# Pooled attention and a token/channel mixer on one core: seven-product stage in one more unit, column-tiled token tails, and a rewritten plan

## The chip, the cores and the metric

The kernel runs on one core of one Trainium2 chip. The metric is device time in microseconds of one execution, median of the runs. Engines: TensorE (PE, with weight loads shown as PEld), VectorE (DVE), ScalarE (ACT), GpSimd (POOL), and SyncE (SP), which only issues DMAs here.

## The reference

Eight batches, eight heads, 576 tokens, head size 64. Keys and values are averaged over groups of eight tokens, so that each head attends to 72 keys. The result feeds a mixer: a token layer across the 576 tokens (hidden size 256), then a channel layer across the 512 channels (hidden size 1536), each with a residual.

```
k_p = k.reshape(B, H, Sp, 8, D).mean(axis=3);  v_p likewise
attn = softmax(scale * q @ k_p^T);  x = (attn @ v_p) as (B, S, H*D)
h = relu(x^T @ w_tok1) @ w_tok2;    u = x + h^T
h2 = relu(u @ w_ch1) @ w_ch2;       return u + h2
```

## The kernel before

A batch's 576 tokens are taken as four chunks of 128 and a tail of 64. The work of a batch is cut into named steps: `k0`, `k1`, `v0`, `v1` pool half of the heads on VectorE and `K0` to `V1` the same on GpSimd (`pool`, `pool8`); `kq` pools K on PE by multiplying with the identity (`ppool`); `kpT` transposes the pooled K; `Q0`, `Q1` turn q; `s0` to `s2` are scores and exponentials, eight matmuls tiled by 32 rows (`score4`); `av0` to `av4` are attention times V with the division; `at0`, `at1` the first token layer; `u0` to `u3` the second token layer with its residual, and `u4` that of the tails of two batches at once; `t` and `r` transpose u on PE (evicted on VectorE or ScalarE), and batches from `BOUNCED` = 6 on are turned by `M0`, `M2` (spill to HBM), `M` (load in quarters) and `T0` to `T3` (32x32 block transposes on VectorE).

Batch 0 takes other steps in the head, among them `A0` to `A3`, which finish its transposed u with two matmuls of 512 columns each.

The channel layers are done in nine units: unit n is batch n, and unit 8 is all the tails. A unit has two stages. The first (`first_stage` with `l1_tiles`, or `first_fast`) makes the 12 blocks of the hidden layer `GT`, 512 token columns each; in units 3 to 8, for the groups of `GROUPS`, four blocks are made by seven products on half-size operands instead of eight. The second stage is `unit_plain` (48 matmuls of 512 columns) or, from unit `FAST` on, `unit_fast`: seven products of 12 matmuls of 256 columns each, on sums of weights (`T`, made once by `weight_sum`, tokens `W`) and sums of `GT` (`S`, made in each unit by `g_sums`, tokens `=1a` to `=4b`, or `=10` to `=42` by pairs). S[1] is made from S[0], and S[3] from S[1]. S and T lie in two early buffers, `area` and `area2`, that the head uses for other things. The first stage's own sums are of weights (`%`, `in_weight_sum`) and of tokens (`^`, `token_sum`).

K and V of batches 0 to 3 are loaded as bf16 by GpSimd's DMA queue and pooled in three additions. From batch `SUMMED` = 4 on, a first DMA brings two of the eight rows of a group and three more add to it in flight (`add_rows`, tokens `+`), each waiting for the one before; one addition per half is left.

The order is written out by hand: `HEAD` lists the steps up to unit 0, and `PLANS[n]` says after which yield of unit n's stream of matmuls which steps of other batches are put in. A unit of `unit_fast` yields 23 or so times in its first stage and three times for each product after it. Engines run their instructions in that order, and GpSimd's and SP's DMA issues stand in their queues in that order too. A `<` or `>` ahead of a step shifts its batch.

Of the kernel before, what the change touches and what calls it, by code (L numbers as in the profile page):

```python
# [14 lines left out]
SUMMED = 4  # L15
BOUNCED = 6
FAST = 2
# [11 lines left out]
PLANS = {  # L29
# [32 lines left out]
def kernel(  # L62
# [74 lines left out]
    def pair_sums(b, key):  # L137
        return loaded[b, key].rearrange("j h i d -> j (h i d)").bitcast(FP32)[:, 0:H * 2 * D].rearrange(
            "j (h n) -> j h n", h=H)
# [828 lines left out]
```

## Time and profile before

| | |
|---|---|
| Median of 3 runs | 271.58 us (271.04 to 271.66) |
| Profiled execution | span 269.8 us; no other time is given for it |
| PE, DVE, ACT, POOL busy | 259.5, 206.8, 122.7, 113.4 us |
| Granted TensorE clock | 1.000 |
| DMA | 42081 packets, 35.17 MB, mean 130 GB/s |

```profile
PE   8999999999999999999999999999999999999992
...
DVE  4755573751798859996978798899799889997981
...
POOL 5847749999995428636657242420000000000000
```


The columns of the table come from the page's first lines. The two rows above cut the span into 40 equal slices of 6.7 us; a digit is the engine's busy share in tenths. In the page's other parts, a group of instructions has its line, engine, operation, tiles and shapes, then busy us, mean ns, and the idle time ahead of it with what ended it. Start-to-start times of matmuls are read from the chain, since single matmuls overlap.

### The profile page before, as it was taken

The page shows a single profiled execution, that of the slowest core. Times are in us where ns is not written, and L with a number is a line of the kernel's source. Part 1 is how long each engine was busy: PE and PEld are TensorE (multiplying, and loading weights), DVE is VectorE, ACT ScalarE, POOL GpSimd, SP SyncE. Part 2 cuts the span into 40 slices and gives each one's busy share as a digit, 9 for nine tenths or more (in the row PEclk, how much of TensorE's full clock was granted, in tenths as well). Part 3 has the DMA queues.
Part 4 walks back from the last instruction along what each step waited for, and adds up shares of the span by engine and source line. Part 5 has one row for each costly group of instructions (what it writes and reads, how often), then busy time and mean ns, then how long its engine had stood idle before and what let it go on. Part 6 is the DMA issues. An engine that isn't in the chain of part 4 may idle for free.

```text
span 269.8 us, 5432 instructions
## 1 busy us (share of the span) xinstructions
PE 259.5 (96%) x2173; PEld 171.7 (64%) x2200; DVE 206.8 (77%) x427; ACT 122.7 (45%) x207; POOL 113.4 (42%) x114
## 2 busy tenths in 40 slices
PE   8999999999999999999999999999999999999992
PEld 2776454545544645776587657864785688787781
DVE  4755573751798859996978798899799889997981
ACT  1375773047444353736563637264922632613600
POOL 5847749999995428636657242420000000000000
PEclk9999999999999999999999999999999999999999
DMA  7999999959969898998995997361506510404106
GB/s 184 190 194 205 204 212 204 180 126 190 153 132 140 154 159 118 146 169 168 155 141 83 156 213 87 39 164 40 119 0 147 149 18 21 137 2 116 41 2 157
DMA packets 42081, 35.17 MB, mean 130 GB/s; under 512 B 12040, under 2 KB 34408, under 8 KB 42056
## 3 DMA queue, kind: packets, MB, share of 16 engines
q0 software_dynamic: 30672, 22.11, 55.3%
q1 hardware_dynamic: 11056, 12.39, 17.2%
q10 hardware_dynamic: 328, 0.33, 0.5%
q8 instruction: 17, 0.28, 0.4%
q14 instruction: 8, 0.07, 0.1%
HBM read 36.90 MB, written 10.49 MB: 176 GB/s over the span
## 4 chain that ended last, share of the span: by engine, by line
PE 90%; DVE 5%; ACT 2%; issue 1%; DVEq 0%
PE p L777 24%; PE p L561 22%; PE p L695 9%; PE p L592 8%; PE p L453 6%; PE p L468 5%; PE p L357 4%; PE p L391 3%; PE p L862 3%; PE p L480 2%; PE p L323 1%; DVE area L614 1%; DVE u L470 1%; ACT ex L379 1%; ACT x L426 1%
## 5 line engine op out<-in xcount | busy, mean ns | idle before, releaser
L564 ACT ACTIVATE GT<-p 128x512 bf16<-128x512 f32 x76 | 44.5, 596 | 57.6 <-PE p L561 43.7
L561 PE MATMUL p<-uT,w_ch 128*128 128x512 bf16 x274 | 69.3, 380 | 0.9 <-issue 0.4
L561 PEld LDWEIGHTS <-w_ch 128*128 128x128 bf16 x304 | 32.4, 114 | 24.1 <-issue 1.7
L362 ACT ACTIVATE ex<-p 72x1024 bf16<-72x1024 f32 (+1 forms) x42 | 31.6, 804 | 27.5 <-PE p L357 27.3
L777 PEld LDWEIGHTS <-area 128*128 128x128 bf16 x336 | 31.9, 98 | 5.3 <-issue 1.3
L777 PE MATMUL p<-area,area 128*128 128x256 bf16 x252 | 30.8, 273 | 0.0
L145 POOL DMA_DIRECT2D kr<-in_k_dram x16 | 23.4, 1495 | 15.6 <-DMA kr<-in_k_dram 15.6
L145 POOL DMA_DIRECT2D vr<-in_v_dram x16 | 23.1, 1478 | 14.2 <-DMA vr<-in_v_dram 14.2
L470 DVE TENSOR_TENSOR u<-p,x 128x512 bf16<-128x512 f32 x32 | 21.1, 680 | 8.2 <-PE p L468 8.2
L777 PEld LDWEIGHTS <-GT 128*128 128x128 bf16 x252 | 24.2, 98 | 4.9 <-issue 0.6
L592 PE MATMUL p<-w_ch,GT 128*128 128x512 bf16 x92 | 23.6, 379 | 0.2
L777 PE MATMUL p<-w_ch,GT 128*128 128x256 bf16 x168 | 20.6, 273 | 0.1
L799 DVE TENSOR_TENSOR o<-p,s 128x512 f32<-128x512 f32 (+1 forms) x28 | 17.9, 662 | 3.2 <-PE p L777 3.1
L396 DVE TENSOR_TENSOR x<-p,den 128x512 bf16<-128x512 f32 x28 | 19.4, 691 | 1.0
L468 PE MATMUL p<-AT,w_tok 128*128 128x512 bf16 x62 | 17.3, 379 | 0.5 <-DVE u L470 0.5
L799 DVE TENSOR_TENSOR s<-p,u 128x512 f32<-128x512 f32 x24 | 16.2, 680 | 2.0 <-PE p L777 2.0
L395 DVE RECIPROCAL den<-p 128x8 f32<-128x8 f32 (+1 forms) x35 | 7.0, 201 | 11.3 <-PE p L391 10.9
L391 PEld LDWEIGHTS <-ex 72*128 72x128 bf16 x280 | 12.6, 98 | 3.9 <-DVE x L396 0.2
L592 PEld LDWEIGHTS <-GT 128*128 128x128 bf16 x96 | 8.8, 98 | 9.4 <-issue 0.4
L453 PE MATMUL p<-x,w_tok 128*128 128x512 bf16 x53 | 13.7, 379 | 0.2
L446 ACT ACTIVATE AT<-p 128x512 bf16<-128x512 f32 x14 | 8.4, 597 | 12.1 <-PE p L453 11.7
L391 PE MATMUL p<-vp,ex 72*128 72x65 bf16 x280 | 13.7, 194 | 0.0
(151 smaller groups left out, 448.8 us busy)
## 6 DMA issues: line engine op xcount, KB each, us to landing
out_dram<-o SPq DMA_DIRECT2D x34, 256.0 KB, 3.8
kr<-in_k_dram POOLq DMA_DIRECT2D x16, 288.0 KB, 7.4
vr<-in_v_dram POOLq DMA_DIRECT2D x16, 288.0 KB, 7.0
qb<-in_q_dram POOLq DMA_DIRECT2D x7, 576.0 KB, 10.1
kr<-in_k_dram POOLq DMA_DIRECT2D x3, 576.0 KB, 10.9
vr<-in_v_dram POOLq DMA_DIRECT2D x3, 576.0 KB, 12.4
w_ch<-in_moe_w_ch_dram POOLq DMA_DIRECT2D x6, 256.0 KB, 10.6
w_ch<-in_moe_w_ch_dram POOLq DMA_DIRECT2D x3, 512.0 KB, 13.1
```

Of the source, the lines that this page charges most:

```text
L145: nc.gpsimd.dma_start(out=pair_sums(b, key), in_=src[:, :, 2 * i * D:2 * (i + 1) * D], accum_op=ALU.add if i else ALU.bypass)
L362: nc.scalar.activation(out=exv[:, a, :, gs[0]:gs[-1] + 1, n0:n0 + n], func=AF.Exp, scale=scale, in_=pss[a][0:SP, :, 0:len(gs) * n].rearran ...
L391: nc.tensor.matmul(out=ps[:, h // 4, (h % 4) * (D + 1):(h % 4 + 1) * (D + 1)], lhsT=st["ex"][:, h * S + n0:h * S + n0 + P], rhs=st["vp"][: ...
L453: nc.tensor.matmul(out=ps, lhsT=w_tok1[:, c if c < 4 else 4 + par, m * P:(m + 1) * P], rhs=st["x"][:, c, :] if c < 4 else st["xt"], start= ...
L468: nc.tensor.matmul(out=ps, lhsT=w, rhs=a, start=(i == 0), stop=(i == len(mms) - 1))
L470: nc.vector.tensor_tensor(out=quads_of(dst, on), in0=plain_of(ps, on), in1=plain_of(x, on), op=ALU.add)
L561: nc.tensor.matmul(out=ps[m], lhsT=w_ch1[m // 4][:, kk, m % 4:512:4], rhs=moving(u)[kk], start=(kk == 0), stop=(kk == 3))
L564: nc.scalar.activation(out=GT[:, m, :], in_=ps[m], func=AF.Relu)
L592: nc.tensor.matmul(out=ps, lhsT=GT[:, m, c * P:(c + 1) * P], rhs=w_ch2[:, m, :], start=(m == 0), stop=(m == NM - 1))
L695: nc.tensor.matmul(out=ps[:, i], lhsT=w(i, k), rhs=mv(k), start=start and (i, k) == (0, 0), stop=stop and k == 1, skip_group_check=True)
L777: nc.tensor.matmul(out=ps[i] if split else ps[:, i], lhsT=a(m)[:, i * P:(i + 1) * P], rhs=w(m), start=start and m == 0 and (i == 0 or spli ...
L799: nc.vector.tensor_tensor(out=dst, in0=src, in1=other[:, i], op=ALU.add)
```

## The change

- `FAST` = 1: unit 1's second stage is `unit_fast`, so the sums of `w_ch2` are made in unit 1.
- In `unit_fast` the products come in the order GT lo, GT second half, S[1], S[0], S[2], S[3], GT hi; the buffer `s4` and its addition are gone, and the last product adds u directly.
- `u4` uses 64-column tiles of the second token layer's weights at two column positions instead of the zero-padded `w_tok2t`, which is gone.
- `BOUNCED` = 5: batch 5 is turned through HBM too.
- `ROWS`: K and V of batches 4 to 7 come in two DMAs of four rows, the second adding to the first; two additions per half are left.
- K of batch 1 is pooled on VectorE (`k0:1`, `k1:1`), not by `kq0`, `kq1` on PE; the K halves of batches 2 and 3 go from GpSimd to VectorE. `kpA` evicts the transposed keys on ScalarE.
- `#` and `~` do sums of GT and of tokens on GpSimd; `=` and `^` on VectorE as before.
- `HEAD` has 13 warm-up matmuls for 26, K of batch 0's first heads in two smaller DMAs, and another order.
- `PLANS` is replaced throughout; steps name their batch after a colon, and `do` runs them.
- The last unit stores its parts as they come, its last part in two transfers.

The core of the diff, with the plan of a few units:

```
-SUMMED = 4
-BOUNCED = 6
-FAST = 2
+ROWS = {4: 4, 5: 4, 6: 4, 7: 4}
+BOUNCED = 5
+FAST = 1
...
-HEAD = """z Z d2 Lc d5 d2 Lk8 d2 d2 d1 d2 d2 d1 d1 R0 c1 c0 I Lk1 Lq Lv0 Lv8 Lv1 kf0 Lf Lb La R1 d1 kf1 Bk1 H0 d1
-          d4 q1 kt0 kt1 q0 kp2 kp3 o0 e0 kt2 kt3 q2 q3 o1 e1 P0 vp0 o2 e2 a00 a01 a02 vp1 o3 e3 P1 y00 y01 y02 y03
-          y04 b10 X0 X1 a11 a12 A1 A0 y10 y11 y12 y13 y14 X2 X3 Bq1 Bv1 P2 H1 H2 Bk2 Ld G0"""
+HEAD = """Sk0 S80 z Sq0 Sk1 Sq1 N z0 R0 Z Lc d1 d1 d1 d1 d1 d1 d1 d1 d1 d1 d1 d1 d1 I kf0 c0 Lk1 kT0 p0 Lk8 c1 Lq
+          e0 o0 kf1 kt1 Lv8 Lv0 q1 kp2 kt2 Lv1 p3 La Lf kp3 q2 o1 kt3 e1 vP0 e2 e3 o2 a00 a01 vp1 o3 P1 a02 Lb X1
+          X0 Bk1 H0 P0 b10 y00 y01 a12 Bq1 a11 y02 y10 y03 y04 H1 y11 R1 Bv1 X2 A1 k0:1 y12 y13 A0 y14 H2 Ld X3
+          A3:0"""
...
-    1: {1: "s1", 5: "+k3a", 8: "av1", 10: ">K0", 16: ">K1 av2", 17: "av3", 18: "lk4", 20: ">Q0 s2", 21: ">Q1",
-        22: "av0", 23: "av4", 25: ">kpT", 27: "lq4", 29: "at1 >V1 at0", 30: "W10", 34: ">v0 >s1 u1", 35: "u3",
-        37: "W11 >s0 t3 W02 +v3b u0", 40: "u2", 41: "+k3b t0", 42: "W00 t2 >s2", 45: "t1 lv4 %01", 46: "W01 >av4"},
...
+    1: {
+        0: "W00 lv:3", 1: "W12 W02", 3: "W01", 9: "W10 lq:3", 11: "s1:2", 12: "=3a", 13: "W03", 16: "W11",
+        17: "k0:3 k1:3", 18: "=1a s2:2", 21: "av1:2", 23: "kpA:3 =2a", 24: "=1b av0:2", 25: "+v:4 +k:4",
+        28: "#2b av3:2", 29: "av4:2", 30: "#4a", 31: "av2:2", 32: "=3b Q0:3 Q1:3", 33: "W13 V1:3",
+        35: "at1:2 at0:2 =4b lq:5 s0:3", 36: "u1:2", 37: "u3:2", 38: "s2:3", 39: "u2:2 s1:3 t3:2 V0:3", 40: "u0:2",
+        41: "r2:2", 42: "r0:2 lq:4", 43: "t1:2 av4:3",
+    },
+    2: {
...
+    4: {
+        1: "at0:5 Q0:6 at1:5 Q1:6", 3: "k0:6", 4: "^14 K1:6 u2:5 u0:5 u1:5", 6: "Q0:7", 7: "~24", 10: "t4:1",
+        11: "M0:5 %61", 12: "V0:6 ~34 kpA:6", 15: "u3:5", 19: "=3b V1:6 lv:7 =3a =1a", 20: "s0:6", 21: "#2a",
+        23: "=1b", 25: "s2:6 u4:5", 26: "#2b", 27: "s1:6", 29: "#4b", 32: "av4:6 M2:5", 34: "av0:6", 35: "#4a M:5",
+        37: "T0:5", 38: "r4:3 T2:5 T1:5", 39: "T3:5 %62 av2:6", 43: "+v:7 av3:6",
+    },
+    5: {
...
+    8: {
+        2: "~38", 17: "=11", 18: "=12 =32", 21: "=21 =22", 22: "=10 =20", 26: "#30 =31", 27: "#40", 36: "#41 #42",
+    },
...
-    w_tok2t = singles.tile([P, 2, 2, P], BF16)
...
-        nc.gpsimd.dma_start(out=pair_sums(b, key), in_=src[:, :, 2 * i * D:2 * (i + 1) * D],
+        nc.gpsimd.dma_start(out=pair_sums(b, key), in_=src[:, :, ROWS[b] * i * D:ROWS[b] * (i + 1) * D],
...
-                if b < SUMMED:
+                if b not in ROWS:
                     pool8(eng, loaded[b, t], hs, dst, t == "k")
                     return
-                pair = pair_sums(b, t)[:, hs].rearrange("j l (i n) -> i j l n", i=2)
+                rows = pair_sums(b, t)[:, hs]
+                if ROWS[b] == 4:
+                    eng.tensor_tensor(out=rows[:, :, 0:2 * D], in0=rows[:, :, 0:2 * D], in1=rows[:, :, 2 * D:4 * D], op=ALU.add)
+                pair = rows[:, :, 0:2 * D].rearrange("j l (i n) -> i j l n", i=2)
...
-        def kpT():
+        def kpT(act=False):
...
+            (nc.scalar.copy if act else nc.vector.tensor_copy)(
+                out=st["kD"].rearrange("p g e j -> p (g e j)"), in_=ps.rearrange("p i j -> p (i j)"))
...
-                    mms = [(w_tok2t[:, m, half, :], tails[b // 2, half][:, m, :]) for half in range(2) for m in range(2)]
+                    mms = []
                     dst, x = u_tails[:, b // 2, :], st["xt"]
+                    for m in range(2):
+                        for half in range(2):
+                            rows = slice(half * BP, (half + 1) * BP)
+                            nc.tensor.matmul(out=ps[rows], lhsT=w_tok2[:, m, 8 * BP:S], rhs=tails[b // 2, half][:, m, :],
+                                             start=(m == 0), stop=(m == 1), tile_position=(0, half * BP))
...
+    def sub(out, a, b, eng=nc.vector):
+        eng.tensor_tensor(out=out, in0=a, in1=b, op=ALU.subtract)
...
-    def token_sum(n, u, i):
+    def token_sum(n, u, i, eng):
...
-        def store_part(cols):
-            def go(i):
-                if i == 0:
-                    return
-                for half in range(2):
-                    dst = out.rearrange("(c h) (p r) n -> h p c r n", h=2, r=BR)[half]
-                    (nc.scalar if half else nc.sync).dma_start(out=dst[:, 2:4, 8, cols],
-                                                               in_=ob[half * BP:(half + 1) * BP, :, cols])
-            return go
+        def store_part(g, o, cols, i):
+            for half in range(2):
+                dst = out.rearrange("(c h) (p r) n -> h p c r n", h=2, r=BR)[half]
+                (nc.scalar if half else nc.sync).dma_start(out=dst[:, 2 * g:2 * g + 2, 8, cols][:, i],
+                                                           in_=o[half * BP:(half + 1) * BP, i, cols])
...
-        yield from product(y, lambda m: GT[:, NH + m, lo], lambda m: w_ch2[:, NH + m, lo], True, plus(oa[:, :, lo], y, s1))
+        both = slice(0, 2)
+
+        def stored(g, o, cols):
+            return (lambda i: i == 0 or store_part(g, o, cols, both)) if last else None
+
+        yield from product(y, lambda m: GT[:, NH + m, lo], lambda m: w_ch2[:, NH + m, lo], True,
+                           plus(oa[:, :, lo], y, s1, stored(0, oa, lo)))
+        s2 = keep("s1")
+        yield from product(x, lambda m: SG[:, 1, m], lambda m: TW[:, 1, m], False, plus(s2, x, u1hi), last)
         z = bank()
         s5 = keep("s5")
         yield from product(z, lambda m: SG[:, 0, m], lambda m: TW[:, 0, m], True, plus(s5, z, u2hi))
-        s2 = keep("s1")
-        yield from product(x, lambda m: SG[:, 1, m], lambda m: TW[:, 1, m], False,
-                           plus(s2, x, u1hi), last)
+        yield from product(x, lambda m: SG[:, 2, m], lambda m: TW[:, 2, m], False,
+                           plus(ob[:, :, hi], x, s5, stored(1, ob, hi)), last)
+        yield from product(z, lambda m: SG[:, 3, m], lambda m: w_ch2[:, NH + m, hi], False,
+                           plus(oa[:, :, hi], z, s2, stored(0, oa, hi)))
         if not last:
-            w = bank()
-            s4 = keep("s4")
-            yield from product(w, lambda m: GT[:, NH + m, hi], lambda m: TW[:, 3, m], True, plus(s4, w, u2lo))
-        yield from product(z, lambda m: SG[:, 3, m], lambda m: w_ch2[:, NH + m, hi], False, plus(oa[:, :, hi], z, s2))
-        store(n, 0, oa)
-        if last:
-            yield from product(x, lambda m: SG[:, 2, m], lambda m: TW[:, 2, m], False,
-                               plus(ob[:, :, hi], x, s5, store_part(hi)), True)
-            yield from product(x, lambda m: GT[:, NH + m, hi], lambda m: TW[:, 3, m], False,
-                               plus(ob[:, :, lo], x, u2lo, store_part(lo)), True)
-        else:
-            def finish(i):
-                plus(ob[:, :, hi], x, s5)(i)
-                plus(ob[:, :, lo], x, s4)(i)
-            yield from product(x, lambda m: SG[:, 2, m], lambda m: TW[:, 2, m], False, finish)
+            store(n, 0, oa)
+        yield from product(x, lambda m: GT[:, NH + m, hi], lambda m: TW[:, 3, m], False,
+                           plus(ob[:, :, lo], x, u2lo, (lambda i: store_part(1, ob, lo, i)) if last else None), last)
+        if not last:
             store(n, 1, ob)
...
+        elif s[0] == "S":
+            a = int(s[2])
+            if s[1] == "q":
+                nc.sync.dma_start(out=qf[:, a:a + 1, :], in_=q_pairs(a, a + 1))
+            elif s[1] == "8":
+                kv(kf, k, 0, 0, HP, BP, SP, nc.scalar)
+            else:
...
+    def do(s):
+        if s[0] == "W":
+            weight_sum(int(s[1]), int(s[2]))
+        elif s[0] == "%":
+            in_weight_sum(int(s[1]), int(s[2]))
+        elif s[0] in "^~":
+            b = int(s[2])
+            token_sum(b, batches[b][2] if b < B else dict(uT=uT_tails), int(s[1]), nc.vector if s[0] == "^" else nc.gpsimd)
+        elif s[0] in "=#":
+            g_sums(s[1:], nc.vector if s[0] == "=" else nc.gpsimd)
```

More of the change, by code (lines that the diff above doesn't have):

```diff
@@ L137, in pair_sums @@
     def pair_sums(b, key):
-        return loaded[b, key].rearrange("j h i d -> j (h i d)").bitcast(FP32)[:, 0:H * 2 * D].rearrange(
+        return loaded[b, key].rearrange("j h i d -> j (h i d)").bitcast(FP32)[:, 0:H * ROWS[b] * D].rearrange(
             "j (h n) -> j h n", h=H)
@@ L187, in permute_tok2 @@
             return
-        for half in range(2):
-            nc.gpsimd.tensor_copy(out=w_tok2t[:, :, half, half * BP:(half + 1) * BP], in_=w_tok2[:, :, 8 * BP:S])
     def load_ch1(g):
@@ L338, in go @@
                                         in_=loaded[b, "q"][:, hp, rr * P:(rr + 1) * P], identity=ident)
-                nc.vector.tensor_copy(out=qT0[:, hp].rearrange("m l (r p) -> m r l p", p=BP), in_=ps)
+                (nc.scalar.copy if act else nc.vector.tensor_copy)(
+                    out=qT0[:, hp].rearrange("m l (r p) -> m r l p", p=BP), in_=ps)
             return go
@@ L890, in head @@
             nc.vector.memset(w_tok1[:, 4:6, :], 0.0)
-            nc.vector.memset(w_tok2t, 0.0)
         else:
             batches[0][1][s]()
+    def do(s):
[8 more added lines that the diff above has]
+            g_sums(s[1:], nc.vector if s[0] == "=" else nc.gpsimd)
+        elif ":" in s:
+            s, b = s.split(":")
+            if s[0] == "l":
+                load(s[1], int(b))
+            elif s[0] == "+":
+                add_rows(int(b), s[1])
+            else:
+                batches[int(b)][1][s]()
+        else:
+            head(s)
     def unit(n, at):
@@ L903, in unit @@
             for s in at.get(i, "").split():
-                if s[0] == "W":
-                    weight_sum(int(s[1]), int(s[2]))
-                    continue
-                if s[0] == "%":
-                    in_weight_sum(int(s[1]), int(s[2]))
-                    continue
-                if s[0] == "^":
-                    b = int(s[2])
-                    token_sum(b, batches[b][2] if b < B else dict(uT=uT_tails), int(s[1]))
-                    continue
-                if s[0] == "!":
-                    head(s[1:])
-                    continue
-                if s[0] == "=":
-                    g_sums(s[1:])
-                    continue
-                if s[0] == "l":
-                    load(s[1], n + int(s[2]))
-                    continue
-                if s[0] == "+":
-                    if SUMMED <= n + int(s[2]) < B:
-                        add_rows(n + int(s[2]), s[1])
-                    continue
-                ahead = {"<": 0, ">": 2}.get(s[0], 1)
-                s = s.lstrip("<>")
-                if n + ahead < B and ((n + ahead) % 2 or s not in ("u4", "t4", "r4")):
-                    batches[n + ahead][1][s]()
+                do(s)
     with tc.manual_schedule(engines={PE, POOLE, DVE, ACT, SYNC}):
@@ L934 @@
         for s in HEAD.split():
-            head(s)
+            do(s)
         for n in range(B + 1):
```

44 lines of the change are left out of this document (26 added, 18 removed), and 45 rows, old and new, of the table PLANS.

## The prediction

> **What bounds the kernel now.** I read the page first, then the stages, the waits of TensorE, the chain of waits, the groups by shape and the timeline at a few places.
>
> ```profile
> PE 259.5 (96%) x2173; PEld 171.7 (64%) x2200; DVE 206.8 (77%) x427; ACT 122.7 (45%) x207; POOL 113.4 (42%) x114
> ...
> PE 90%; DVE 5%; ACT 2%; issue 1%; DVEq 0%
> ```
>
> TensorE (PE) is busy for 259.5 of 269.8 us and carries 90% of the chain that ended last. A busy share can hide waits inside pipelined matmuls, so I look at stages (start:end, share of PE, weight loads, VectorE, ScalarE, GpSimd in us) and at the waits of PE.
>
> ```profile
> 0.00:23.45 23.45, 20.95 (x189) 13.89 (x191) 14.15 (x43) 11.26 (x23) 15.62 (x29) 1.00 1.07 192
> 23.45:58.85 35.40, 34.79 (x253) 18.40 (x256) 20.79 (x39) 15.03 (x24) 27.44 (x25) 1.00 1.08 196
> 58.85:89.14 30.29, 29.92 (x236) 15.01 (x238) 19.76 (x36) 14.99 (x24) 25.02 (x20) 1.00 0.92 149
> 89.14:119.10 29.96, 29.25 (x253) 19.09 (x256) 25.77 (x51) 14.68 (x24) 17.21 (x15) 1.00 1.00 137
> ...
> 175.27:205.31 30.04, 29.93 (x273) 19.86 (x275) 28.01 (x57) 16.33 (x28) 1.60 (x2) 1.00 0.34 86
> ```
>
> ```profile
> PE p L862 <- DVE area L881: 1.2, 1, 1.2
> PE p L413 <- ACT ex L379: 0.6, 2, 0.4
> PE p L468 <- DVE u L470: 0.5, 1, 0.5
> ```
>
> The stretches are head, units 0, 1, 2 and 5. From unit 0 on PE misses at most 0.7 us in a unit, and its longest wait for another engine after the head is 0.5 us. In unit 5 VectorE is busy for 28.01 of 30.04 us and PE still does not wait. So what a removed matmul is worth is its place in the stream, start to start, and what other engines gain or lose is worth nothing until one falls behind PE. The chain gives those places:
>
> ```profile
> 24.91 0.88 PE p L323 x8
> ...
> 54.70 0.58 PE p L357 x8
> ...
> 57.54 0.45 PE p L480 x8
> ...
> 98.82 0.88 PE p L468 x4
> ...
> 131.01 2.16 PE p L561 x10
> ...
> 217.43 9.17 PE p L777 x84
> ```
>
> A 512-column matmul takes 2.16/10 = 0.216 us, a 256-column one 0.109 to 0.110, a 128-column transpose 0.056.
>
> **The change part by part.** The plan is rewritten as a whole, so I take PE's removed work term by term and then ask of each other engine whether it keeps up. The counts come from comparing the two instruction streams.
>
> *Seven products in unit 1.* 48 matmuls of 512 columns (L592) become 84 of 256: 48 x 0.216 = 10.37 against 9.17 from the row of 84. Gain 1.2 us. VectorE pays three more output adds (7 for 4) and eight sums of GT halves, of which six stay on it; the eight sums of w_ch2 were made before too, only later. Unit 1 has the room: 19.76 busy of 30.29.
>
> *K of batch 1 off TensorE.* 16 matmuls of 256 columns with the identity (L323, kr) go: 2 x 0.88 = 1.76 us. VectorE gets two half pools of three operations instead of two copies.
>
> *Batch 5 turned via HBM.* 16 transposes go: 2 x 0.45 = 0.9 us. The turn adds two spills, four loads on SP's queue and four 32x32 block transposes on VectorE. Batches 6 and 7 do the same now and their units start without a wait, so I cost it at nothing else. SP's queue holds only stores beside it.
>
> *Token tails.* Four times, four matmuls with a zero-padded weight (0.88 us on the chain) become two pairs of 64-column tiles. Nothing in this trace is tiled by columns; the nearest row is the scores', tiled by rows: eight 512-column matmuls in 0.58 us, where two rounds of four would be 0.43 and one after another 1.73. So tiles overlap and a change of tiling costs about 0.15. For a pair-wise tail that is 0.43 + 0.15 = 0.58, a gain of 0.30 each and 1.2 in all. The ends are 4 x 0.43 = 1.7 gained if the change of tiling is free, and 4 x 0.15 = 0.6 lost if the pairs do not overlap. I take 1.1, since the two halves feed different moving data through the same rows, which the scores do not do. The Trainium skill, TensorE: Matmul & The Clock Gate, Part 3, gives 2.38 times the speed for three column tiles; two at that efficiency (an estimate) would be 1.6 times, 0.55 us a tail, 1.3 gained. The Trainium skill, TensorEngine Tiling (Array Packing), Restrictions, speaks against: column tiling switches the fast weight load off. No row here shows that; weight loads overlap other matmuls, so the sum does not use it.
>
> *The head.*
>
> ```profile
> 5.75 1.14 DVE L302 TENSOR_TENSOR GT<-GT 72x512 f32<-72x512 f32 x2 [2.53 <-DMA GT<-in_k_dram]
> ...
> 9.58 0.44 PE L337 MATMUL p<-ident,qb 128*128 128x128 bf16 x5
> ...
> 12.64 0.71 POOL L194 DMA_DIRECT2D w_ch<-in_moe_w_ch_dram  x1 [1.00 <-DMA vr<-in_v_dram]
> ...
> 23.45 0.59 PE L561 MATMUL p<-uT,w_ch 128*128 128x512 bf16 x2
> ```
>
> ```profile
> w_ch<-in_moe_w_ch_dram POOLq DMA_DIRECT2D x6, 256.0 KB, 10.6
> ```
>
> The K of the first heads comes in two smaller loads and PE's first useful work needs only the first, with 13 warm-up matmuls for 26: perhaps 3 us sooner than 9.58. But the DMA engines are full in this stage (share 1.07), and unit 0 needs w_ch1, whose second load was issued at 12.64 and takes a median of 10.6: about 23.2. Unit 0 began at 23.45, and some steps of batch 0 stood after that (two of the A steps, 0.86 us), which can now be done before. The gain lies between nothing and some 2.5 us; I take 0.7, nearest to the row of w_ch1.
>
> *K and V from two halves.* 32 accumulating loads of two rows become 16 of four.
>
> ```profile
> L145 POOL DMA_DIRECT2D kr<-in_k_dram x16 | 23.4, 1495 | 15.6 <-DMA kr<-in_k_dram 15.6
> ...
> L218 POOL TENSOR_TENSOR t<-t 72x512 f32<-72x512 f32 x8 | 10.3, 1288 | 0.7
> ...
> L217 POOL TENSOR_TENSOR t<-vr 72x1024 f32<-72x1024 bf16 x4 | 8.5, 2133 | 1.8 <-DMA vr<-in_v_dram 1.7
> L277 POOL TENSOR_TENSOR vp<-vr 72x256 bf16<-72x256 f32 x8 | 8.5, 1067 | 6.1 <-DMA vr<-in_v_dram 6.1
> ...
> L614 DVE TENSOR_TENSOR area<-GT 128x768 bf16<-128x768 bf16 x10 | 6.1, 611 | 0.0
> ...
> L217 DVE TENSOR_TENSOR t<-vr 72x1024 f32<-72x1024 bf16 x2 | 3.5, 1745 | 0.0
> ...
> L221 POOL TENSOR_TENSOR kp<-t 72x256 bf16<-72x256 f32 x4 | 3.3, 836 | 0.3
> ...
> L614 DVE TENSOR_TENSOR area<-GT 128x512 bf16<-128x512 bf16 x6 | 2.5, 416 | 0.7 <-ACT GT L564 0.7
> ...
> L218 DVE TENSOR_TENSOR t<-t 72x512 f32<-72x512 f32 x2 | 1.8, 896 | 0.1
> ...
> L223 DVE TENSOR_TENSOR vp<-t 72x256 bf16<-72x256 f32 x2 | 0.8, 424 | 0.1
> ```
>
> GpSimd saves 16 issues x 1.495 = 24 us, and its waits for landings get fewer. It pays ten more adds of 512 elements, 13 us.
>
> *Replaced work.* GpSimd loses the K pools of batches 2 and 3 (four halves, 2.13 + 1.29 + 0.84 = 4.3 us each) and gets 24 sums of GT and 14 token sums: 19 of 768 elements at about 1.7 (between 1.288 and 2.133), 19 of 512 at 1.29, 57 us. Its total comes to about 113 - 24 + 13 - 17 - 6 (six pair adds of 1.07 that go to VectorE) + 57 = 136 of some 265 us, now spread over all units. VectorE gives those 38 sums (19 x 0.61 + 19 x 0.42 = 20 us), six score-key copies and six output adds, and takes the six K half pools of batches 1 to 3 (1.745 + 0.896 + 0.42 = 3.1 each, 18 us), six adds of later halves and four block transposes. Its sum changes by about 2 us. Unit by unit, with these prices, I get VectorE at 31 against PE 32 in unit 0, 28 against 29 in unit 1, 24 to 26 against 27 to 29 in units 2 to 5, 16 against 21 in unit 6: tightest early, looser than before from unit 4 on (unit 5 was 28.01).
>
> *The new order in the second layer.* The product on S[1] moves one product (1.31 us) forward, while its second half needs a chain: last relu on ScalarE, a sum on VectorE (0.61), and in units 1 and 4 a sum on GpSimd (1.7). In unit 1 that is
>
> ```profile
> L564 ACT ACTIVATE GT<-p 128x512 bf16<-128x512 f32 x76 | 44.5, 596 | 57.6 <-PE p L561 43.7 <-DVE o L799 8.9 <-issue 4.4
> ```
>
> the last matmul 0.2, the relu 0.6, the sums 0.6 and 1.7, plus hand-overs, 3.5 to 4, against two products and three attention steps on PE, 2.6 + 0.8 = 3.4, so a wait of 0 to 0.5 there; behind it stand all later matmuls of the unit. In unit 4 two more score steps lie before it. In unit 8 the last sums of S[3] run on GpSimd, three of 1.29 in a row against 6.5 us of PE work. I charge 0.6 for such waits in all.
>
> *The end.*
>
> ```profile
> 264.62 0.42 DVE L799 TENSOR_TENSOR o<-p,u_tails 128x256 f32<-128x256 f32 x1 [0.23 <-PE p L777]
> ```
>
> ```profile
> out_dram<-o SPq DMA_DIRECT2D x2, 128.0 KB, 3.8
> ```
>
> The last product stays, and its last store of 128 KB is halved; from that add to the end 269.8 are 5.2 us, of which a smaller transfer may save 0.1.
>
> **Sum.** 1.2 + 1.76 + 0.9 + 1.1 + 0.7 + 0.1 - 0.6 = 5.2 us off the span: 269.8 - 5.2 = 264.6. The page gives the profiled execution by its span alone; the median of the timed runs, 271.58, is 1.8 over it. With the same 1.8 the forecast is 266.4.
>
> **The rivals.**
>
> *VectorE falls behind PE because GpSimd holds it up (slower).* This is the strongest objection:
>
> ```profile
> 100.29 2.09 POOL L277 TENSOR_TENSOR kp<-kr 72x256 bf16<-72x256 f32 x2 [4.63 <-DMA kr<-in_k_dram]
> ...
> 101.60 1.19 DVE L614 TENSOR_TENSOR area<-GT 128x768 bf16<-128x768 bf16 x1
> ...
> 105.09 0.55 DVE L614 TENSOR_TENSOR area<-GT 128x768 bf16<-128x768 bf16 x1
> ```
>
> The same sum takes 0.55 alone and 1.19 beside a GpSimd sum: both read SBUF twice, and each waits for the other. After the change GpSimd computes for roughly a third of the time (136 us less some 50 of DMA issues, of 265), and VectorE has some 60 us of such SBUF operations (40 sums of GT and 10 of tokens, 26 us; eight half pools alone at about 2.3, 19; six later halves, 7; weight sums, 10): a third of 60, about 20 us of lengthening. Spread out, VectorE still stays under PE. It decides from the point at which it comes together in unit 1 (28 us of VectorE against 29 of PE, with w_ch2 sums, K pools and two V pools of GpSimd side by side): 6 us more there is 34 against 29, 5 us of waiting, and 1 us in each of units 3 to 5: 8 us, so 266.4 + 8 = 274.4. The Trainium skill, GPSIMD Engine Reference, Engine selection and Key points, advises the same way: two-input elementwise work belongs on VectorE, GpSimd is about twice as slow and shares SBUF interfaces with it. By that rule, the trace agrees (1.7 to 0.55, and the 1.19). Against it: unit 5 ran at 28.01 of 30.04 with no wait of PE.
>
> *The small gains fail (still faster).* Column tiles do not overlap, the head keeps w_ch1's date, and PE waits 1.5 us for sums: 1.2 + 1.76 + 0.9 - 0.6 + 0.1 - 1.5 = 1.9 off, 269.7.
>
> *The head gives all it could (faster).* If the earlier first work and the freed queue bring unit 0 forward by 2.5 us: 266.4 - 1.8 = 264.6; with free tiling changes and no waits for sums 263.4.
>
> *Unit 1's seven products wait for their weights' sums.* If the third load of w_ch2, which now is queued behind K of batch 2, delays unit 0's second layer, or the sums in `area2` are late by about 5 us, nothing is left: 271.6. The bytes ahead of that load are the same as before, which speaks against it.
>
> **How the numbers follow.** Forecast 0.57, around 265 to 268; small gains fail 0.14; head gives all 0.10; unit 1's weights 0.05; VectorE behind 0.14. A measurement of this kernel tells a change from none at about 0.3%, 0.8 us. Faster by more than that: 0.57 + 0.14 + 0.10 = 0.81, of which I move 0.02 to slower for waits that no row shows; so 0.79 faster, 0.05 same, 0.16 slower. The range runs from 263.0, a little under the head's best case, to 271.0, just short of no change, and leaves out about 0.2.
>
> **What would show it.** In the profile after: no L323 on kr for batch 1; 84 more 256-column matmuls in unit 1 and none of 512 at the plain layer beyond unit 0; each tail at about 0.6 us on the chain; PE's waits after the head below 0.5 us each and its busy sum down by 5 or more; unit 0's first matmul of the channel layer between 21 and 23.5. I am wrong if PE waits for VectorE or GpSimd by more than 3 us in units 1 to 5, if L614 and the pools on VectorE lengthen to over 1.0 us on average, or if unit 0 starts later than 23.5.

## The result: 1.0 us gained of the 5.2 forecast

The median over 20 runs each is 270.55 us after (268.19 to 272.95) against 271.58 before (270.51 to 272.64). The ratio is 0.9949, 95% interval 0.9929 to 0.9969: 0.5% faster, far less than forecast. The three longest executions after (272.23 to 272.95) belong to a slower state and are not in the ratio. The profiled execution of the changed kernel is the longest of its 20, 272.95 us with a span of 271.1; why shows below. The page after:

```profile
PE 258.2 (95%) x2191; PEld 173.3 (64%) x2191; DVE 216.6 (80%) x415; ACT 125.2 (46%) x213; POOL 133.7 (49%) x126
...
PEclk9856999999999999999999999999999999999999
```

GpSimd's sum came out as worked out (133.7 for about 136). New is the row of the granted clock, full in every slice of before. The stages after, units 0 to 4 in the same columns as in the prediction, with the granted clock third from the right:

```profile
0.00:30.32 30.32, 24.17 (x179) 16.86 (x180) 15.60 (x42) 14.13 (x27) 17.49 (x30) 0.77 1.08 187
30.32:63.49 33.17, 32.61 (x233) 15.81 (x232) 27.71 (x46) 14.01 (x24) 11.99 (x11) 1.00 1.03 183
63.49:93.30 29.81, 29.19 (x275) 18.27 (x274) 26.81 (x48) 17.75 (x29) 21.44 (x19) 1.00 0.85 138
93.30:121.61 28.31, 28.31 (x257) 18.37 (x255) 22.81 (x46) 14.23 (x23) 16.20 (x15) 1.00 0.88 177
121.61:150.88 29.27, 28.25 (x280) 19.82 (x279) 26.83 (x46) 14.01 (x23) 22.43 (x20) 1.00 0.86 155
```

Unit 0 begins at 30.32 instead of 23.45, and the clock in the head is 0.77. From there to TensorE's last matmul it takes 236.3 us instead of 241.1, and from that to the end 4.4 instead of 5.2: nearly all that was hoped for is there, and the head takes 6.9 back. The timeline of TensorE in the head (start, length, then the idle time before and what ended it):

```profile
4.58 1.30 PE L887 MATMUL p<-area 128*128 128x512 bf16 x5
6.20 0.30 PE L337 MATMUL p<-ident,area 72*128 72x72 bf16 x4 [0.32 <-DVE area L329]
...
7.58 0.65 PE L401 MATMUL p<-area 128*72 128x320 bf16 x4 [0.80 <-ACT area L364]
...
10.43 0.61 PE L317 MATMUL p<-kr,ident 72*72 72x128 bf16 x8 [1.69 <-DMA kr<-in_k_dram]
11.55 0.42 PE L337 MATMUL p<-ident,area 72*128 72x72 bf16 x4 [0.52 <-DVE area L320]
12.26 0.71 PE L362 MATMUL p<-ident,qb 128*128 128x128 bf16 x5 [0.29 <-DMA qb<-in_q_dram]
```

The warm-ups (L887) end before 6 us, and in the next 6.5 us TensorE waits five times, 3.6 us in all, for K, q and their evictions. The clock records of this trace read: 1.0 for 6.83 us from 4.68, then 0.5 for 13.65 us from 11.51, then 1.0 to the end. Before there was one record, 1.0. Executions differ in how much of this they have: mean clocks and times of four runs after are 1.000 and 268.19 us, 0.991 and 268.83, 0.984 and 271.02, 0.975 and 272.95.

### The profile page after: what moved, and what is told of

It reads as the page before. It is cut to its first block, busy times and chain, and to the rows that moved or that the text cites. A ratio compares the mean times of both kernels' runs of the same rounds, so it can differ in the third digit from the quotient of the medians.

```text
span 271.1 us, 5481 instructions
## 1 busy us (share of the span) xinstructions
PE 258.2 (95%) x2191; PEld 173.3 (64%) x2191; DVE 216.6 (80%) x415; ACT 125.2 (46%) x213; POOL 133.7 (49%) x126
## 4 chain that ended last, share of the span: by engine, by line
PE 80%; DVE 13%; DMA 2%; issue 1%; POOL 1%; ACT 0%; DVEq 0%
PE p L808 23%; PE p L592 22%; PE p L726 8%; PE p L499 5%; PE p L479 5%; PE p L623 4%; PE p L383 3%; PE p L417 3%; DMA qb<-in_q_dram 2%; DVE o L830 2%; PE p L511 2%; DVE t L695 1%; DVE x L422 1%; PE p L348 1%; PE p L401 1%
## 5 line engine op out<-in xcount | busy, mean ns | idle before, releaser
L808 PEld LDWEIGHTS <-area 128*128 128x128 bf16 x384 | 35.9, 98 | 6.2 <-issue 0.9
L808 PE MATMUL p<-area,area 128*128 128x256 bf16 x288 | 36.1, 273 | 0.0
L808 PEld LDWEIGHTS <-GT 128*128 128x128 bf16 x288 | 27.1, 98 | 7.6 <-issue 2.5
L645 POOL TENSOR_TENSOR area<-GT,area 128x768 bf16<-128x768 bf16 (+1 forms) x12 | 17.7, 1492 | 26.0 <-DVE area L645 26.0
L808 PE MATMUL p<-w_ch,GT 128*128 128x256 bf16 x192 | 24.0, 273 | 0.0
L830 DVE TENSOR_TENSOR o<-p,s 128x512 f32<-128x512 f32 (+1 forms) x25 | 16.5, 664 | 4.9 <-PE p L808 4.6
L645 POOL TENSOR_TENSOR area<-area,GT 128x768 bf16<-128x768 bf16 x4 | 6.5, 1632 | 25.4 <-DVE area L656 25.4
L645 POOL TENSOR_TENSOR area<-GT 128x768 bf16<-128x768 bf16 (+1 forms) x7 | 11.5, 1649 | 12.2 <-ACT GT L595 6.7
L830 DVE TENSOR_TENSOR s<-p,u 128x512 f32<-128x512 f32 x21 | 14.4, 686 | 3.4 <-PE p L808 3.4
L417 PEld LDWEIGHTS <-ex 72*128 72x128 bf16 x280 | 13.5, 98 | 3.3
L656 DVE TENSOR_TENSOR area<-GT 128x768 bf16<-128x768 bf16 (+1 forms) x17 | 8.5, 507 | 6.8 <-ACT GT L595 6.8
L808 PE MATMUL p<-w_ch,area 128*128 128x256 bf16 x96 | 12.8, 273 | 0.3 <-DVE area L645 0.3
```

What stands on the lines that cost most here:

```text
L417: nc.tensor.matmul(out=ps[:, h // 4, (h % 4) * (D + 1):(h % 4 + 1) * (D + 1)], lhsT=st["ex"][:, h * S + n0:h * S + n0 + P], rhs=st["vp"][: ...
L645: eng.tensor_tensor(out=out, in0=a, in1=b, op=ALU.subtract)
L808: nc.tensor.matmul(out=ps[i] if split else ps[:, i], lhsT=a(m)[:, i * P:(i + 1) * P], rhs=w(m), start=start and m == 0 and (i == 0 or spli ...
L830: nc.vector.tensor_tensor(out=dst, in0=src, in1=other[:, i], op=ALU.add)
```

## The experiments

Four questions, a comparison of three or four kernels for each: what the clock costs; where the gain of the head and of unit 0 went; what each piece of removed matmul work is worth; which version is best. My theory to begin with was the clock; the rivals were the order of the head and VectorE held up by GpSimd. The kernel before, run beside them, took 271.52, 271.58, 271.27 and 271.39 us in the four comparisons.

### The clock

**26 warm-ups again**, in a row, all else as in the change:

```
-... Lc d1 (13 times) I kf0 ...
+... Lc d1 (26 times) I kf0 ...
```

> The changed kernel with 26 warm-up matmuls in a row for 13; they end near 8.3 us instead of 5.5. Clock theory (the shorter warm-up leaves TensorE idle in the head, its clock is halved for one or two periods of 6.8 us and unit 0 starts late): granted clock 1.000 in every run, unit 0's first matmul of the channel layer near 25 us instead of 30.3, time 266.5 to 268. Rival (the new head's order and its loads make it late, the clock follows from that and costs little): clock may rise, but time stays 269.5 to 271.

Measured: 269.08 us, ratio 0.9909 [0.9886, 0.9932]; clocks 0.997 to 1.0. The head and unit 0:

```profile
0.00:25.20 25.20, 20.68 (x192) 13.74 (x194) 15.38 (x42) 13.81 (x27) 16.13 (x28) 1.00 1.07 189
25.20:58.36 33.16, 32.39 (x229) 15.82 (x232) 27.70 (x46) 14.01 (x24) 13.38 (x13) 1.00 1.15 207
```

The rest is as after, to 0.02 us in each unit up to unit 6. Of the 6.9 us that the profiled head lost, 5.1 are the clock; over all executions it is 270.55 - 269.08 = 1.5. But unit 0 still begins at 25.20.

**The gaps filled**: 13 early warm-ups kept, 15 more put where TensorE waited, so that no real work comes later.

```
-Lq e0 o0 kf1 kt1 Lv8 Lv0 q1 kp2 kt2 Lv1 p3
+Lq d4 e0 o0 kf1 kt1 Lv8 Lv0 q1 d7 kp2 d2 kt2 Lv1 d2 p3
```

> The changed kernel with 15 more warm-up matmuls, put where TensorE waits in the head (4 before the first scores, 7 before the first K pool on TensorE, 2 and 2 after it). Clock theory: clock 1.000, and as they fill waits only, 266 to 267.5, as fast as with 26 in a row or a little faster. Rival (order and loads): 269.5 to 271, as the late loads are not touched.

Measured: 268.90, ratio 0.9900 [0.9877, 0.9923]; clocks 0.998 to 1.0. Unit 0 begins at 25.61. Both ways of keeping TensorE busy bring the clock back, so idleness it is. Neither brings unit 0 to 23.5.

**The other way round**: the kernel before with its last 13 warm-ups dropped.

```
-d2 d2 d1 d2 d2 d1 d1 R0 ... R1 d1 kf1 Bk1 H0 d1 d4 q1
+d2 d2 R0 ... R1 kf1 Bk1 H0 q1
```

> The kernel before with 13 of its 26 warm-up matmuls (the later ones left out), nothing else. Clock theory: TensorE idles from about 5.5 to 9.4 us, the clock is halved for some runs, 272.5 to 275.5 and a wide scatter. Rival: no loss, 271 to 272, since its order of the head is untouched.

Measured: 271.86, ratio 1.0012 [0.9993, 1.0032]; clocks 0.982 to 0.996. Its trace has a wait of 2.2 us behind the warm-ups and one half-clock record of 6.83 us (7.88 to 14.7). So the halving is not special to the new plan. In the profile unit 0 begins 1.3 later than in the kernel before; in the medians it costs only 0.3 us, within what can be told from nothing.

**The head of before** on the new kernel, with its warm-ups and its order (one larger K load excepted, which the new steps take in two):

```
-HEAD = """Sk0 S80 z Sq0 Sk1 Sq1 N z0 R0 Z Lc d1 ... X0 Bk1 H0 P0 b10 ... H2 Ld X3 A3:0"""
+HEAD = """z Sk0 Sk1 S80 Sq0 Sq1 N z0 Z d2 Lc d5 d2 Lk8 ... X2 X3 Bq1 Bv1 k0:1 H1 H2 Ld A3:0"""
```

> The changed kernel with the order and warm-ups of the head before (26 warm-ups, both copies of q first), the split loads and the steps that the new plan needs kept. Clock theory: clock 1.000, unit 0 near 23 to 24 us, 266 to 267.5. Rival: the same, and 2 us or more faster than the new head with 26 warm-ups or filled gaps.

Measured: 268.93, ratio 0.9912 [0.9889, 0.9935], the same as with 26 warm-ups alone. Unit 0 begins at 24.71 and ends at 58.73, where it ended at 58.36 with the new order and at 58.69 in the kernel before. In the medians the order of the head decides nothing. The end of unit 0 has hardly moved, though 2.8 us of matmul work and waiting were to go from the head and unit 0; how long the warm-ups themselves took in each profile is in these ends too, and is reckoned with further down.

### Where the gain of unit 0 went

With the gaps filled, the third load of `w_ch2` is late, as one of the rivals had it, but by 0.8 us, not 5 (waits of TensorE: total, count, longest):

```profile
PE p L623 <- DMA w_ch<-in_moe_w_ch_dram: 0.8, 1, 0.8
```

**That load ahead of K of batch 2**, the gaps filled as before (all of this comparison starts from it):

```
-7: "u3:0 G1", ... 20: "av2:1 G2"
+7: "u3:0 G1 G2", ... 20: "av2:1"
```

> The kernel with filled gaps, and the third load of w_ch2 issued ahead of K of batch 2, not behind it. Theory (with a full clock the rest of the missing gain is TensorE waiting 0.8 us or more in unit 0's second stage for that load): the wait in front of L623 goes, 267.5 to 268.3, and no new wait for K of batch 2. Rival (the 1 us of scatter comes from elsewhere): 268.9 as with filled gaps alone.

Measured: 271.76, ratio 1.0011 [0.9987, 1.0036]: 2.9 us lost. The wait for `w_ch` is gone, and this stands in its place, in the timeline of VectorE and in the waits of TensorE:

```profile
49.54 1.22 DVE L238 TENSOR_TENSOR t<-kr 72x1024 f32<-72x1024 bf16 x1 [2.83 <-DMA kr<-in_k_dram]
...
54.40 0.69 DVE L501 TENSOR_TENSOR u_tails<-p,xt 128x512 bf16<-128x512 f32 x1
```

```profile
PE p L499 <- DVE u_tails L501: 2.3, 1, 2.3
```

K of batch 2 lands later, VectorE waits 2.83 us for it with both half pools at the head of its queue, and the eviction that TensorE needs stands behind these until 54.40. In the kernel before, GpSimd pooled this K, and its waiting held up no eviction.

**The tails padded again**, with `w_tok2t` back, on the same kernel:

```
-nc.tensor.matmul(out=ps[rows], lhsT=w_tok2[:, m, 8 * BP:S], rhs=tails[b // 2, half][:, m, :], ...
+mms = [(w_tok2t[:, m, half, :], tails[b // 2, half][:, m, :]) for half in range(2) for m in range(2)]
```

> As with w_ch2 early, but the token tails of two batches again in one zero-padded matmul each. If the column tiles overlap as the trace says (four matmuls in about 0.55 us for 0.86), this is 1.2 us slower than the run with w_ch2 early; if TensorE has slack in those units, less than 0.5.

Measured: 272.32, ratio 1.0038 [1.0011, 1.0066], 0.6 over the kernel it starts from, with overlapping intervals. The profiles are sharper: units 2, 4 and 6 are 0.32, 0.31 and 0.20 us longer, the other units from 1 on the same to 0.01.

**All sums on VectorE**: the 24 sums of GT and 14 of tokens that GpSimd had taken.

```
-28: "#2b av3:2", 29: "av4:2", 30: "#4a", ...   41: "~23",
+28: "=2b av3:2", 29: "av4:2", 30: "=4a", ...   41: "^23",
```

> As with w_ch2 early, but the 24 sums of GT and 14 token sums of GpSimd are back on VectorE, at the same places of the order. Theory A (GpSimd's sums hold VectorE up and cost TensorE 1 to 3 us in units 1 and 3): faster by 0.5 to 2 us. Theory B (VectorE would be the bound without that help): slower by 2 us or more, with waits for VectorE in units 4 to 8.

Measured: 287.36, ratio 1.0575 [1.0528, 1.0621]: 15.6 us more. Its page and the waits of TensorE:

```profile
PE 262.0 (92%) x2206; PEld 171.4 (60%) x2206; DVE 234.0 (82%) x453; ACT 125.0 (44%) x213; POOL 83.0 (29%) x88
```

```profile
PE p L808 <- DVE area L645: 3.8, 4, 1.4
PE p L499 <- DVE u_tails L501: 3.6, 1, 3.6
```

VectorE is busy only 82% of the span, and TensorE waits for it all the same. This trace also has two stretches of 3.41 us at half clock, from 54.9 and from 85.7 us, so at most 3.4 of the 15.6 are the clock. GpSimd's help is what carries the new plan.

**Three steps moved** where VectorE was late in units 0, 1 and 3:

```
-1: "G0 A2:0 kpT:1"                      +1: "G0 A2:0", 3: "kpT:1"
-32: "=3b Q0:3 Q1:3" 35: "... =4b lq:5"  +32: "=3b Q0:3" 34: "=4b" 36: "Q1:3 lq:5 ..."
-8: "%21" (unit 3)                       +27: "%21" (unit 2)
```

> As with w_ch2 early, and three steps moved: the transposes of batch 1's keys two yields later, the last sum of S[3] ahead of the second turn of q in unit 1, one sum of w_ch1 from unit 3 to unit 2. The stalls seen in the trace (0.6 in unit 0, about 1.2 in unit 1, 1.2 in unit 3) should go: 1.5 to 2.5 us faster than with w_ch2 early, 265.5 to 266.5. Rival (they only move on to the next wait): under 0.5 us.

Measured: 269.16, ratio 0.9914 [0.9882, 0.9946], 2.6 us under the kernel it starts from. Unit 1 fell from 29.81 to 28.83 us, unit 3 from 29.26 to 28.09, and unit 2 rose from 28.31 to 29.15, 1.3 in sum; the other 1.3 of the profile lies ahead of unit 1, which begins at 61.14 for 62.46. What VectorE and GpSimd did in units 1 and 3 is in the timeline of the kernel with the gaps filled:

```profile
81.33 2.14 POOL L238 TENSOR_TENSOR t<-vr 72x1024 f32<-72x1024 bf16 x1
...
81.52 2.37 DVE L645 TENSOR_TENSOR area<-GT,area 128x768 bf16<-128x768 bf16 x1
...
83.95 0.28 PE L808 MATMUL p<-w_ch,area 128*128 128x256 bf16 x1 [0.31 <-DVE area L645]
...
84.55 0.38 PE L499 MATMUL p<-AT,w_tok 128*128 128x512 bf16 x1 [0.32 <-DVE u L501]
```

```profile
122.26 2.43 DVE L695 TENSOR_TENSOR t<-w_ch,w_ch 128x512 bf16<-128x512 bf16 x1
...
122.97 1.17 POOL L645 TENSOR_TENSOR t<-uT,t 128x512 bf16<-128x512 bf16 x1
...
125.59 0.38 PE L479 MATMUL p<-x,w_tok 128*128 128x512 bf16 x1 [1.03 <-DVE x L422]
```

A sum of 0.55 us alone takes 2.37 beside GpSimd's V pool, and in the lines behind it TensorE waits. In unit 3 it is `%21`, a sum of weights that could be made at another time, ahead of the eviction of x. This is the slower rival's mechanism, at about 2 us in two units instead of 8 in four.

### What each piece is worth

**More moves**, on the last kernel: K of batch 2 pooled four or five yields later, `A2:0` ahead of `k1:1`, `%21` in the middle of unit 2.

```
-28: "av4:1 k1:2 lv:2", 29: "at1:1 at0:1 k0:2"   +28: "av4:1 lv:2", ... 32: "k1:2", 34: "k0:2 lk:3"
-0: "k1:1", 1: "G0 A2:0"                         +0: "A2:0", 1: "G0 k1:1"
-27: "%21" (unit 2)                              +14: "%21" (unit 2)
```

> Filled gaps, w_ch2 early, the local moves, and two more: VectorE pools K of batch 2 four to five yields later, so that its wait for that load has fewer evictions behind it, and batch 0's last A step goes ahead of the pool of batch 1's K. Theory (a late load costs TensorE only by what stands behind the waiting instruction in VectorE's queue): the waits of 2.3 us in unit 0 and 0.7 in unit 2 go, 265.8 to 267.0, the fastest version. Rival (the loads themselves are late for TensorE): 268 to 269.

Measured: 270.78, ratio 0.9989 [0.9965, 1.0012]. A miss. Unit 2 is at 28.31 with `%21` in it, as expected, but the later pools cost more in unit 0 than they gave:

```profile
PE p L499 <- DVE o L631: 2.2, 1, 2.2
PE p L307 <- DVE kp L242: 1.7, 1, 1.7
```

It is the base of the next three.

**Unit 1's second stage plain**, with the sums of w_ch2 made in it still:

```
-FAST = 1    (unit 1: "=3a", "=1a", "=2a", "=1b", "#2b", "#4a", "=3b", "=4b")
+FAST = 2    (unit 1: none of these)
```

> As all moves, with unit 1's second layer in 48 matmuls of 512 columns and without its eight sums of GT. Predicted term: 1.2 us slower than all moves. If VectorE and GpSimd were what limits unit 1, it is less than 0.5 slower or even faster.

Measured: 272.95, ratio 1.0038 [1.0014, 1.0061], 2.2 over its base. Unit 1 takes 30.02 us for 28.83: 1.19, the predicted 1.2 to a hundredth. The rest of the difference lies in unit 0, in which this edit changes nothing: this trace has half clock for 3.41 us there, from 57.29 to 60.70, just behind TensorE's wait of 2.2 us for VectorE, and the base's trace, with the same wait, has none. Eight of the 12 executions here have a mean clock of 0.994 or less, and four of the base's 12; the medians of the others, 271.3 and 270.4, are 0.9 apart.

**K of batch 1 on TensorE again**:

```
-... A1 k0:1 y12 ...   0: "A2:0", 1: "G0 k1:1"
+... A1 kq0:1 y12 ...  0: "A2:0", 1: "G0 kq1:1"
```

> As all moves, with K of batch 1 pooled by TensorE again (16 matmuls of 256 columns and two copies) and not on VectorE. Predicted term: 1.8 us slower than all moves. If VectorE's pools stand in the way in unit 0, it is less than 0.8 slower.

Measured: 270.88, ratio 0.9993 [0.9970, 1.0016]: 0.1 more than its base. The 1.76 us of removed matmuls bring nothing here.

**Batch 5 turned on TensorE again**:

```
-BOUNCED = 5   11: "M0:5 %61" 32: "av4:6 M2:5" 35: "#4a M:5" 37: "T0:5", 38: "r4:3 T2:5 T1:5", 39: "T3:5 ..."
+BOUNCED = 6   11: "%61"      32: "av4:6"      35: "#4a"     37: "r0:5", 38: "r4:3 r2:5 t1:5", 39: "t3:5 ..."
```

> As all moves, with batch 5 turned by 16 transposes on TensorE and two evictions each on ScalarE and VectorE, not via HBM. Predicted term: 0.9 us slower than all moves.

Measured: 273.44, ratio 1.0068 [1.0039, 1.0097], 2.7 over its base. This trace too has half clock for 3.41 us in unit 0. Unit 4, where the turn stands, takes 28.45 us for 26.95: 1.50, against 0.9 predicted.

### The best version

Still open by then was whether the head, or K of batch 1, or VectorE's lateness kept the gain; these two leave the loads and unit 0 as the change has them.

**26 warm-ups, and only the moves in units 1 to 3**:

```
-Lc d1 (13 times) I                      +Lc d1 (26 times) I
-32: "=3b Q0:3 Q1:3" 35: "... =4b lq:5"  +32: "=3b Q0:3" 34: "=4b" 36: "Q1:3 lq:5 ..."
-8: "%21" (unit 3)                       +14: "%21" (unit 2)
```

> The changed kernel with 26 warm-ups in a row and the moves in units 1 to 3 alone (last sum of S[3] ahead of the second turn of q, one sum of w_ch1 into unit 2's first stage); unit 0 and the loads as in the change. Theory (the waits in units 1 and 3 were VectorE's queue, and unit 0 is best left as it was): 2.2 us faster than 26 warm-ups alone, 266.5 to 267.3. Rival (unit 0's wait for loads takes back what comes earlier): 268.0 to 268.8.

Measured: 267.59, ratio 0.9842 [0.9818, 0.9866]: the fastest here, ahead of both kernels, and 1.5 under 26 warm-ups alone, where 2.2 were expected. Units 1 to 3 in its stages:

```profile
59.64:88.47 28.83, 28.40 (x271) 18.37 (x274) 25.53 (x48) 17.74 (x29) 20.50 (x18) 1.00 0.88 138
88.47:118.34 29.87, 28.31 (x253) 18.35 (x255) 25.95 (x47) 14.24 (x23) 17.59 (x16) 1.00 0.92 172
118.34:146.42 28.08, 27.92 (x277) 19.86 (x279) 24.37 (x45) 14.01 (x23) 21.93 (x20) 1.00 0.92 165
```

Unit 2 has a wait of 1.4 us (L808 for one of VectorE's additions, L830) that the earlier kernel with the same `%21` did not show, so there is a little more to be had.

**The same, K of batch 1 on TensorE**:

```
-... A1 k0:1 y12 ...   0: "k1:1"
+... A1 kq0:1 y12 ...  0: "kq1:1"
```

> As with the moves in units alone, but K of batch 1 pooled by TensorE, in the places of the plan as changed. Predicted term: 1.8 us slower than the moves in units alone. If what TensorE saves there is lost to waits for VectorE's pools and for the loads of unit 0, under 0.6 slower.

Measured: 268.18, ratio 0.9877 [0.9852, 0.9902]: 0.6 more, with overlapping intervals.

## Why the prediction was wrong

**The head (0.7 gained; lost instead).** This is the step that failed. I took the row of `w_ch1`, which lands at about 23.2, as what sets unit 0, and asked only what TensorE could begin sooner, not what it would do between its early start and its next loads. The sum has no term for the clock. Two things followed. TensorE waits 3.6 us in the head, and the clock halves, for 13.65 us in the profile: 1.5 us of the median, 5.1 of the profiled execution, shown by filling the time in two ways. The Trainium skill, TensorE: Matmul & The Clock Gate, Part 1, has the array throttled to half after an idle window of about 3.4 us; here no gap was longer than 1.69, and the granted clock fell all the same, so scattered gaps are enough.

And at full clock unit 0 begins at 24.7 to 27.0 in all versions, later than the 23.45 of before. How much later can't be read off these starts alone, because the 26 warm-ups themselves take more or less time from execution to execution. They start 0.43 us apart until the clock is full and 0.216 from then on, and the clock is full from 6.82 us in the trace of before, from 3.97 with 26 warm-ups. In the chains of the two (start, length):

```profile
1.19 8.55 PE p L862 x26
```

```profile
1.19 7.14 PE p L887 x26
```

The fastest version has the same head. In its profile the clock is full from 6.58 us and the warm-ups take 8.43, 1.29 more, and unit 0 begins 1.28 later; it takes 33.16 us in both:

```profile
0.00:26.48 26.48, 21.96 (x192) 14.07 (x194) 15.29 (x42) 13.82 (x27) 16.17 (x28) 1.00 1.06 185
26.48:59.64 33.16, 32.39 (x229) 15.81 (x232) 27.71 (x46) 14.02 (x24) 13.39 (x13) 1.00 1.14 204
```

Counted from the end of the warm-ups (9.74, 8.34 and 9.62 us), unit 0 begins after 13.71 us in the kernel before and after 16.86 in both of these: 3.15 later, 0.4 of it for the one A step that stands ahead of the start now. TensorE is busy for 12.4 of the 13.71 us and for 13.5 of the 16.86, so 2.0 of the 3.15 is more idle time, in short waits for ScalarE and VectorE; the waits of the kernel with 26 warm-ups have these, all from the head:

```profile
PE p L401 <- ACT area L364: 0.8, 1, 0.8
...
PE p L463 <- ACT x L452: 0.5, 1, 0.5
PE p L337 <- DVE area L320: 0.5, 1, 0.5
PE p L401 <- ACT ex L405: 0.5, 1, 0.5
PE p L549 <- ACT AT L467: 0.5, 1, 0.5
```

With the old order of the head, counted alike, unit 0 begins after 15.38 us (24.71 less 9.33), 1.5 sooner, but ends only 0.6 sooner (after 49.40 us for 50.02), and the medians show no gain. Why the new order waits more was not tested.

**K of batch 1 (1.76; 0.1 and 0.6 in the medians).** The matmuls went, as counted. I costed the pools on VectorE at nothing, as they fit into unit 0's sum. What they do to the order I did not follow, though the first part says that a removed matmul is worth its place in the stream only until another engine falls behind. The timelines of VectorE and TensorE at the start of unit 0, with 26 warm-ups:

```profile
24.82 1.23 DVE L238 TENSOR_TENSOR t<-kr 72x1024 f32<-72x1024 bf16 x1
...
26.80 0.42 DVE L242 TENSOR_TENSOR kp<-t 72x256 bf16<-72x256 f32 x1
27.15 0.68 DVE L551 CAST uT<-p 128x512 bf16<-128x512 f32 x1
```

```profile
27.28 0.24 PE L307 MATMUL p<-ident,kp 72*128 72x72 bf16 x2 [0.56 <-DVE kp L242]
```

The pool of three operations stands between two evictions of uT, and TensorE waits 0.56 for it where it would have computed 0.88; with K on TensorE this wait is gone.

Still, most of the term is there in unit 0 itself, which shrank from 35.24 to 33.16 us: 2.1, where this term, the tail and the moved A step make 1.76 + 0.3 + 0.4 = 2.5. In the profiles of the last two runs, too, the stretch from the end of the warm-ups to the end of unit 0 is 1.66 longer with K on TensorE (51.68 for 50.02). What takes it back there is the wait of 1.4 us in unit 2, which of the two only the one with K on VectorE has; whether that wait belongs to the change is not shown. So the term's worth stays open, between 0.1 and 1.7.

Together: the end of unit 0 was to come 1.76 + 0.7 + 0.3 = 2.8 us earlier. With 26 warm-ups it came 0.3 earlier in the profile (58.36 for 58.69) and, counted from the end of the warm-ups, 1.1 later (50.02 for 48.95). Of the 3.8 missing, about 3.4 are the head's: 0.7 not gained, and 2.7 lost beside the moved A step.

**The seven products (1.2; 1.19), the tails (1.1; about 0.3 each), batch 5 (0.9; 1.50).** These were counted from matmuls in the middle of a stream that TensorE fills, and hold. The chain after has the four matmuls of a tail at the estimate of 0.58 less a little:

```profile
52.66 0.55 PE p L496 x4
```

Of the other 0.6 of batch 5, 0.3 is a wait in unit 4 for ScalarE's eviction of the tails (L511 for L512); the rest was not followed up.

**Waits for sums (0.6; about 2.2).** The moves gave 0.97 in unit 1 and 1.2 in unit 3. In unit 1 I had looked for the wait at the product on S[1], for the sum behind the last relu. It came later, when VectorE's sum for S[3] was held up by GpSimd. Unit 3 I had not looked at.

From unit 1's start to TensorE's end the parts promise 1.2 + 0.9 + 3 x 0.3 - 0.6 = 2.4, and 26 warm-ups measure 205.9 - 203.2 = 2.7: right in sum, though the waits were 1.6 longer than charged: batch 5's 0.6 more is a part of what made up for them, and the rest was not followed up.

**The end (0.1; 0.8).** From the last matmul to the end 5.2 us became 4.4. Before, the last transfers of 128 KB landed 3.8 us after their issue; the rows of the transfers after:

```profile
out_dram<-o SPq DMA_DIRECT2D x3, 128.0 KB, 2.5
...
out_dram<-o SPq DMA_DIRECT2D x2, 64.0 KB, 2.4
```

**Of the three signs that I am wrong**, only the start of unit 0 came true. TensorE's waits for VectorE and GpSimd in units 1 to 5 are 1.6 us after, not over 3:

```profile
PE p L479 <- DVE x L422: 1.0, 1, 1.0
...
PE p L499 <- DVE u L501: 0.3, 1, 0.3
PE p L808 <- DVE area L645: 0.3, 1, 0.3
```

Nor did the sums of GT and the pools on VectorE lengthen that much on average; only four sums of GT did, and GpSimd's took 1.64 where about 1.7 had been estimated between two rows of before:

```profile
L645 POOL TENSOR_TENSOR area<-GT,area 128x768 bf16<-128x768 bf16 x8 | 13.0, 1636 | 9.6 <-DVE area L645 9.5
...
L238 DVE TENSOR_TENSOR t<-kr 72x1024 f32<-72x1024 bf16 x6 | 7.3, 1215 | 0.1
...
L656 DVE TENSOR_TENSOR area<-GT 128x768 bf16<-128x768 bf16 x11 | 6.1, 555 | 6.7 <-ACT GT L595 6.7
...
L645 DVE TENSOR_TENSOR area<-GT,area 128x768 bf16<-128x768 bf16 x4 | 5.6, 1412 | 0.0
```

So the rule of the Trainium skill that I had weighed for the slower rival (GPSIMD Engine Reference, Engine selection and Key points: such sums on VectorE) would have been the wrong guide: its two observations, slower and in the way, show in the rows, but following it costs 15.6 us, because the evictions that TensorE needs stand in VectorE's queue too, behind the sums.

**The books.** The measured median is 270.55 - 266.4 = 4.2 over the forecast. The half clock is 1.5 of it. Up to the end of unit 0, counted from the end of the warm-ups, 2.76 + 1.07 = 3.8 are missing; 0.3 more were gained behind it and 0.7 at the end. That makes 1.5 + 3.8 - 1.0 = 4.3. The profiled span with 26 warm-ups, 265.9, is only 1.3 over the 264.6 of the forecast because its warm-ups took 1.4 us less than those in the profile of before: that execution is its kernel's fastest (267.82 us for a median of 269.08). The loads differ between executions too: the kernel with the gaps filled waits 0.8 for one in its profile.

## What to carry to other kernels

A gain from removed matmuls is sure where TensorE fills its stream (three such terms held to within 0.1 or came out above), and has to be proved where other engines and loads set the pace, as at the start. Ask of each step that is handed to VectorE not only whether its sum fits into the stage, but what stands behind it in its queue and which load it waits for: a pool that waits for a load blocks every eviction behind it. Warm-up work at the start is judged by what follows it: look for the idle time up to the first long stretch of matmuls, and fill it. Two profiles are best compared from the end of the warm-ups, since the time of the same 26 matmuls moved by 1.4 us here.

## What the runs showed of the hardware

- The granted clock fell to half after gaps of 0.3, 0.8, 1.7 and 0.5 us within the 5.7 us up to 11.55, for 13.65 us, and in the kernel before with 13 warm-ups at one gap of 2.2, for 6.83. In unit 0 of two kernels it fell for 3.41 us, within 0.6 us after a wait of 2.2; their base had the same wait and full clock. Why one execution has such a stretch and another none isn't shown; nothing here controlled it.
- At the start of an execution the clock was full from 3.97 us on in one trace (26 warm-ups) and from 6.82 in another (before), and 26 warm-ups took 7.14 to 8.55 us; with one and the same head this moved the start of unit 0 by all of the difference.
- Two 64-column tiles overlap although they take different moving data: four 512-column matmuls in 0.55 us.
- A 768-element sum on VectorE took 2.37 us beside a GpSimd addition of f32 results, and a 512-element sum of weights 2.43 beside GpSimd's, where five of the eight of its kind took 0.68 to 0.69; the pair seen in the trace of before was 1.19 against 0.55.
